# Batch 0 of a linear-attention and MLP kernel: k's first pair loaded ahead of q, w1's first block in row halves, key products by pairs

## The chip, the cores and the metric

The kernel runs on one core of a Trainium2 chip. The metric is device time in microseconds (us) of one execution. Three runs of the kernel before gave 266.63, 266.06 and 266.3 us, median 266.3 us.

Engines are named as in the profile: PE (TensorE, matrix products), PEld (its weight loads), DVE (VectorE), ACT (ScalarE), POOL (GpSimd), SP (SyncE). DMAs are issued from queues of SP, ACT and POOL.

## The reference

```python
q_s = exp(q - max(q, -1)); q_s /= sum(q_s, -1) + 1e-9      # q, k, v: (8, 8, 576, 64), over the head dim
k_s = exp(k - max(k, 2));  k_s /= sum(k_s, 2) + 1e-9       # over the 576 rows
kv  = einsum('bhsd,bhse->bhde', k_s, v)
att = einsum('bhsd,bhde->bhse', q_s, kv)                   # (8, 8, 576, 64)
x   = att.transpose(0, 2, 1, 3).reshape(8, 576, 512)
xn  = (x - mean(x)) / sqrt(var(x) + 1e-6) * g_ln           # over the 512 columns
out = x + relu(xn @ w_ch1) @ w_ch2                         # w_ch1 512 x 2048, w_ch2 2048 x 512
```

Inputs and output are float32.

## The kernel before

The eight batches are worked through in order. Of each, 512 rows make four tiles `t` of 128 rows; the 64 rows that are left of every batch are gathered and make a ninth pass. A pass is an attention part (exponentials on ACT, sums and scalings on DVE, products on PE) and an MLP: `mm1` products with `w1` into `ph`, relu into `hT`, products with `w2` into `pc`, and an output step. While PE works on the MLP of one batch, the attention of the next is laid between its matmuls. The order on every engine is the order in which the code issues instructions: `run(main, side)` walks over the MLP's steps, each with a weight, and issues a side step when the sum of weights has reached the side step's number. From batch 2 on a scheme with seven products in place of eight is used; nothing of it is touched.

Nothing can be laid beside the attention of batch 0, since no MLP is there yet. It is written out by hand in `first_batch` (lines 892 to 993):

- **Loads.** SP issues `load_q0(0)`, which is the half of q for tiles 0 and 1 (L905, 512 KB), then k in four pieces of 288 KB (L916). Piece `j` holds the two heads of pair `j`, with nine rows to a partition. POOL issues v in three pieces (L935: pairs 0 and 1, pair 2, pair 3), the other half of q, then `w1` in two pieces of 256 columns (`w_raw` in the profile, L93) and three of 512, then `w2`, then batch 1.
- **Queries.** `exp_qt(0, t)` on ACT (L198); `norm_q` on DVE (sum L207, reciprocal L250, product L859); `eq_pT` is four transposes on PE into `ptr` (L864) and a copy of `ptr` to `eqT` (L866 on ACT, L868 on DVE).
- **Keys.** `exp_k0(j)` on ACT (L271); `z0_mm(j)`, 18 small matmuls with ones (L279); `recip_z` (L287); `kv0_mm(j)`, 18 small matmuls of the exponentials with v into a PSUM tile `pkv` that two pairs share (L296). Behind the second pair of a tile, two products on DVE write `kv_sb` (L302).
- **Attention out.** `po_half(t, half)` (L402) makes 256 columns of x of tile `t`, from pairs 0 and 1 (`half` 0) or 2 and 3 (`half` 1): two matmuls into `po`, then a copy to `x` on ACT that also sums the row (L407, an ACTIVATE and a read of its accumulator). `sum_halves` adds two such sums on DVE (L414).
- **First x.** `xn_out` on DVE (L380), four transposes (L987), two products with the column `g_col` on DVE into `xnT` (L988). Then comes the first `mm1_part` (L456). `g_columns` (L889, L890) makes `g_col`.
- **warm(n)** issues n matmuls on zeros (L798). Nobody reads what they write.

PSUM has two pools, `att_ps` with two buffers and `mm_ps` with six. A new tile of a pool takes a buffer whose last reader it then waits for. `pkv` and `po_half(t, 0)` are in `att_ps`, `po_half(t, 1)` is in `mm_ps`:

```python
pool, tag = (mm_ps, "m") if half else (att_ps, "a")
po = pool.tile([P, DM], FP32, tag=tag, name="po")
```

The order at the end of the attention part:

```python
recip_z()
for j in range(NP):
    kv0_mm(j)
warm(2)
po_half(0, 0)
warm(3)
po_half(0, 1)
po_half(1, 0)
po_half(1, 1)
sum_halves(0)
```

The MLP of batch 0 begins with matmuls on `w1` columns 0 to 511 and tiles 0 and 1, in `parts` of `mlp_steps`, a tile at a time. Tiles 2 and 3 are made as side steps (`q0_rest`, `x_fast`, `xn_pT`).

Of the kernel before, what the change touches and what calls it, by code (L numbers as in the profile page):

```python
# [12 lines left out]
FP32 = mybir.dt.float32  # L13
# [7 lines left out]
def kernel(  # L21
# [69 lines left out]
    def load_w1(n0, n=512):  # L91
        cols = slice(n0, n0 + n)
        nc.gpsimd.dma_start(w1_sb[:, :, cols], w1_src[:, :, cols])  # L93
# [173 lines left out]
    def exp_k0(j):  # L267

        if j == 0:
            eks[0] = raw.tile([P, NP, T0, D], BF16, tag="kt", name="ek0", bufs=1)  # L270
        nc.scalar.activation(eks[0][:, j], raws[0][0][:, j], AF.Exp)  # L271
# [79 lines left out]
    def po_mm(c, t, i):  # L351


        if i == 0:
            pool, tag = (mm_ps, "m") if c == 0 and t >= 2 else (att_ps, "a")
            pobox["p"] = pobox[c, t] = pool.tile([P, DM], FP32, tag=tag, name="po")
        if c < B:
            nc.tensor.matmul(  # L358
                pobox["p"][:, i * P : i * P + P], eqTs[c][:, t, i, :], kv_sb[:, c, i, :],
                start=True, stop=True,  # L360
            )
        else:
            for half in range(2):
                ps = slice(64 * half, 64 * half + 64)
                nc.tensor.matmul(  # L365
                    pobox["p"][ps, i * P : i * P + P], eqTs[c][:, t, i, ps],
                    kv_sb[:, 2 * t + half, i, :], start=True, stop=True,
                )
# [79 lines left out]
    def mm1_part(c, m, t0, tn, ko):  # L448

        if (m, t0, ko) == (0, 0, 0):  # L450
            new_h()
        half, at = divmod(t0, 2)
        if m % 2 == 0 and at == 0 and ko == 0:
            hbox["ph", m // 2] = mm_ps.tile([P, 2, 2, P], FP32, tag="m", name="ph")
        ph = hbox["ph", m // 2]
        nc.tensor.matmul(  # L456
            ph[:, m % 2, at : at + tn], (w1g if c else w1_sb)[:, ko, m * P : (m + 1) * P],
            xnTs[c][:, t0 : t0 + tn, ko, :],
            start=(ko == 0), stop=(ko == KO1 - 1),
        )  # L460
        if m % 2 == 1 and at + tn == 2 and ko == KO1 - 1:
            dst = hbox["h"][:, m - 1 : m + 1, 2 * half : 2 * half + 2]
            if c == 0 and half and (m // 2) % 2 == 1:
                nc.vector.tensor_scalar_max(dst, in0=ph, scalar1=0.0)
            else:
                nc.scalar.activation(dst, ph, AF.Relu)
# [283 lines left out]
    def mlp_steps(c):  # L750
        if c > FAST:
            return mm1_fast(c) + mm2_fast(c)
        full = range(KO2)
        first, parts = [], ()
        if c == 0:
            full = range(0)
            parts = ((0, 2, 0, 1), (0, 2, 1, 1), (2, 2, 0, 1), (2, 2, 1, 1), (4, 4, 0, 2), (0, 4, 2, 1),
                     (0, 4, 3, 1), (4, 4, 2, 2), (8, 4, 0, 2), (8, 4, 2, 2), (12, 4, 0, 2), (12, 4, 2, 2))
        else:
            full, parts = range(8, KO2), ((0, 8, 0, 2), (0, 8, 2, 2))  # L760
        for m0, mn, t0, tn in parts:
            first += [
                (0.25 * tn, lambda m=m, t0=t0, tn=tn, ko=ko: mm1_part(c, m, t0, tn, ko))
                for m in range(m0, m0 + mn) for ko in range(KO1)
            ]
        first += [(1, lambda m=m, ko=ko: mm1(c, m, ko)) for m in full for ko in range(KO1)]
        if c == 0:
            return first + [
                (1, lambda t=t, ko=ko: mm2_stream(c, t, ko))
                for n in range(4) for t in range(T) for ko in range(4 * n, 4 * n + 4)  # L770
            ]
        if c >= FAST:
            return first + mm2_fast(c)
        return first + [(1, lambda t=t, ko=ko: mm2(c, t, ko)) for t in range(T) for ko in range(KO2)]
# [19 lines left out]
    def warm(n, width=256):  # L794

        w = mm_ps.tile([P, 512], FP32, tag="m", name="warm")
        for _ in range(n):
            nc.tensor.matmul(w[:, 0:width], junk[:, 0:P], junk[:, 0:width], start=True, stop=True)  # L798
# [93 lines left out]
    def first_batch():  # L892

        nc.scalar.preload_act_table_set("natural_log_exp_and_others")
        raws[0] = (
            mlp.tile([P, NP, T0, D], FP32, tag="hT", name="kt0", bufs=1), None,
            raw.tile([P, H, T, D], FP32, tag="qt", name="qt"),
        )
        k0, _, q0 = raws[0]
        v0 = mlp.tile([P, NP, T0, D], BF16, tag="hs", name="v0", bufs=1)  # L900
        raws["v0"] = v0

        def load_q0(half, eng=nc.sync):
            ts = slice(2 * half, 2 * half + 2)
            eng.dma_start(  # L905
                q0[:, :, ts],
                q[0, :, 0:SM, :].rearrange("h (p t) d -> p h t d", t=T)[:, :, ts],
            )

        def src0(x, j, jn):  # L910
            rows = x[0, 2 * j : 2 * j + 2 * jn].rearrange("h (p t) d -> (h p) (t d)", t=T0)
            return rows.rearrange("(j p) n -> p j n", j=jn)

        load_q0(0)
        for j in range(NP):
            nc.sync.dma_start(k0[:, j : j + 1].rearrange("p j t d -> p j (t d)"), src0(k, j, 1))  # L916
        raws["g"] = outp.tile([KO1, P], FP32, tag="ot", name="g_rows")
        nc.scalar.dma_start(
            raws["g"], bass.AP(moe_g_ln.tensor, moe_g_ln.offset, [[P, KO1], [1, P]])
        )  # L920
        nc.vector.memset(junk, 0.0)
        nc.vector.memset(eps_ln, 1e-6)
        nc.vector.memset(ones, 1.0)
        nc.vector.memset(bones, 0.0)
        nc.vector.memset(bones[0:64, 0:1], 1.0)
        nc.vector.memset(bones[64:P, 1:2], 1.0)
        nc.vector.memset(kv_sb, 0.0)
        make_identity(nc, ident)
        nc.gpsimd.tensor_copy(out=ident_f, in_=ident[0:KO1, 0:KO1])
        nc.gpsimd.memset(vr, 0.0)  # L930
        for half in range(2):
            nc.gpsimd.memset(vr[64 * half : 64 * half + 64, :, 4 * half : 4 * half + 4, D:], 1.0)
        nc.gpsimd.memset(vm[:, :, :, :, D:], 1.0)
        for j, jn in ((0, 2), (2, 1), (3, 1)):
            nc.gpsimd.dma_start(  # L935
                v0[:, j : j + jn].rearrange("p j t d -> p j (t d)"), src0(v, j, jn)
            )
        load_q0(1, nc.gpsimd)
        load_w1(0, 256)
        load_w1(256, 256)  # L940
        for nb in range(1, 4):
            load_w1(512 * nb)
        load_w2(0)
        load_w2(1)

        new_eq(0)
        start_x(0)
        warm(31)
        for t in range(2):
            exp_qt(0, t)  # L950
        exp_k0(0)
        exp_k0(1)
        norm_q(0, 0)
        norm_q(0, 1)
        eq_pT(0, 0, nc.scalar)
        g_columns()
        exp_k0(2)
        warm(5)
        z0_mm(0)
        z0_mm(1)  # L960
        exp_k0(3)
        eq_pT(0, 1, nc.vector)
        z0_mm(2)
        warm(3)
        z0_mm(3)
        recip_z()
        for j in range(NP):
            kv0_mm(j)
        warm(2)
        po_half(0, 0)  # L970
        warm(3)
        po_half(0, 1)
        po_half(1, 0)
        po_half(1, 1)
        sum_halves(0)
        exp_qt(0, 2)
        exp_qt(0, 3)
        xn = xs[0][2]
        warm(7)
        for half in range(2):  # L980
            xn_out(0, 0, slice(DH2 * half, DH2 * half + DH2))
        for i in range(2):
            if i:
                warm(2)
            ptr = mm_ps.tile([P, 2, 2 * P], BF16, tag="m", name="ptr")
            for j in range(2):
                nc.tensor.transpose(ptr[:, j, 0:P], xn[:, 0, (2 * i + j) * P : (2 * i + j + 1) * P], ident)  # L987
            nc.vector.tensor_mul(  # L988
                xnTs[0][:, 0, 2 * i : 2 * i + 2], ptr[:, :, 0:P],
                g_col[:, 2 * i : 2 * i + 2].to_broadcast([P, 2, P]),  # L990
            )
        sum_halves(1)
        xn_out(0, 1)
# [36 lines left out]
    with tc.manual_schedule(  # L1030
# [10 lines left out]
        def po_x(c, t):  # L1041
            for i in range(NP):
# [4 lines left out]
            mlp_steps(0),  # L1047
            [
                (2, lambda: (eq_pT(0, 2, nc.scalar), xn_pT(0, 1, nc.vector), eq_pT(0, 3, nc.scalar))),
                (2, lambda: (q0_rest(2), x_fast(0, 2))),  # L1050
                (6, lambda: q0_rest(3)),
                (8, lambda: (xn_pT(0, 2, nc.vector), x_fast(0, 3))),
                (16, lambda: xn_pT(0, 3, nc.vector)),
                (22, lambda: square_sum(0, 0)),
                (26, lambda: square_sum(0, 1)),
# [72 lines left out]
```

## Time and profile before

| | |
|---|---|
| median of three runs | 266.3 us |
| the profiled execution | 266.63 us, of which the span from first to last instruction is 264.8 us and 1.8 us lie around it |
| granted TensorE clock, mean over the span | 0.999 |
| PE busy | 257.6 us, 97% of the span |
| DVE, ACT, POOL busy | 217.0, 175.1, 90.4 us |
| first matmul of the MLP starts | 14.96 us |
| first matmul with w2 starts | 31.53 us |

Times inside the execution are microseconds from the start of the span. In the timeline a row is: start, length, engine, line, operation, what it writes and reads, how many in a row, and in brackets the time that the engine sat idle before it and what ended that. A matmul row's length takes in the drain of its last matmul, so the next row can start before it ends.

### The profile page before, as it was taken

The page shows a single profiled execution, that of the slowest core. Times are in us where ns is not written, and L with a number is a line of the kernel's source. Part 1 is how long each engine was busy: PE and PEld are TensorE (multiplying, and loading weights), DVE is VectorE, ACT ScalarE, POOL GpSimd, SP SyncE. Part 2 cuts the span into 40 slices and gives each one's busy share as a digit, 9 for nine tenths or more (in the row PEclk, how much of TensorE's full clock was granted, in tenths as well). Part 3 has the DMA queues.
Part 4 walks back from the last instruction along what each step waited for, and adds up shares of the span by engine and source line. Part 5 has one row for each costly group of instructions (what it writes and reads, how often), then busy time and mean ns, then how long its engine had stood idle before and what let it go on. Part 6 is the DMA issues. An engine that isn't in the chain of part 4 may idle for free. (4 is left out here: it accounts for less than half of the span.)

```text
span 264.8 us, 6827 instructions
## 1 busy us (share of the span) xinstructions
PE 257.6 (97%) x2708; PEld 217.5 (82%) x2711; DVE 217.0 (82%) x465; ACT 175.1 (66%) x346; POOL 90.4 (34%) x144
## 2 busy tenths in 40 slices
PE   8999999999999999999999999999999999999993
PEld 5778755775988998889888988998899888888882
DVE  4577697968989996999699968996999789877873
ACT  4467851996966886678667866886678378438400
POOL 8742216303059208900880049307300800030000
PEclk9999999999999999999999999999999999999999
DMA  7999999987987995899789997997804530512014
GB/s 226 252 205 207 342 209 329 262 132 255 184 149 221 291 139 101 222 286 143 98 243 268 125 113 235 294 126 155 257 5 84 120 118 5 78 80 81 0 42 119
DMA packets 82328, 45.01 MB, mean 170 GB/s; under 512 B 58036, under 2 KB 78520, under 8 KB 82296
## 3 DMA queue, kind: packets, MB, share of 16 engines
q0 software_dynamic: 32800, 22.29, 45.8%
q1 hardware_dynamic: 48896, 21.76, 40.5%
q10 hardware_dynamic: 600, 0.53, 0.6%
q8 instruction: 21, 0.34, 0.5%
q14 instruction: 11, 0.09, 0.1%
HBM read 36.70 MB, written 9.44 MB: 174 GB/s over the span
## 5 line engine op out<-in xcount | busy, mean ns | idle before, releaser
L548 PEld LDWEIGHTS <-hs 128*128 128x128 bf16 x512 | 49.5, 98 | 5.7
L693 PEld LDWEIGHTS <-w_q 128*128 128x128 bf16 x448 | 43.0, 98 | 6.4 <-issue 1.1
L245 POOL TENSOR_TENSOR tq<-xnT 128x256 bf16<-128x256 bf16 x24 | 15.6, 665 | 76.6 <-DMA xnT<-xn 76.6
L548 PEld LDWEIGHTS <-hT 128*128 128x128 bf16 x384 | 37.2, 98 | 4.4
L693 PEld LDWEIGHTS <-w1g 128*128 128x128 bf16 x336 | 32.2, 98 | 3.9
L548 PE MATMUL ba<-w_q,hs 128*128 128x256 bf16 x256 | 31.7, 273 | 0.0
L693 PE MATMUL bx<-tq,w_q 128*128 128x256 bf16 x224 | 29.4, 272 | 0.2 <-ACT s L721 0.2
L372 ACT ACTIVATE scrap<-x,mv 128x512 bf16<-128x512 bf16 x36 | 25.9, 719 | 1.7 <-DVE x L388 1.3
L717 ACT COPY bc<-bx 128x512 f32<-128x512 f32 x28 | 15.2, 594 | 16.8 <-PE bx L693 16.8
L388 DVE SCALAR_TENSOR_TENSOR x<-po,rq 128x512 bf16<-128x512 f32 x34 | 23.3, 685 | 2.4 <-PE po L358 2.3
L565 POOL DMA_DIRECT2D out_dram<-ot x28 | 15.4, 556 | 24.1 <-DVE ot L559 24.0
L735 ACT ACTIVATE hT<-bc 128x512 bf16<-128x512 f32 x28 | 15.3, 595 | 12.4 <-PE bc L693 12.4
L207 DVE TENSOR_REDUCE zq<-eq 128x16 f32<-128x1024 bf16 (+1 forms) x20 | 20.6, 1049 | 2.0 <-ACT eq L198 2.0
L532 DVE TENSOR_TENSOR hs<-hT 128x1024 bf16<-128x1024 bf16 x32 | 21.3, 674 | 0.9 <-ACT hT L735 0.5
L724 DVE TENSOR_TENSOR bb<-bx,s 128x512 f32<-128x512 f32 x28 | 18.2, 694 | 4.1 <-ACT s L721 4.0
L735 ACT ACTIVATE hT<-bb 128x512 bf16<-128x512 f32 x28 | 15.2, 595 | 9.2 <-PE bb L693 9.2
L358 PE MATMUL po<-kv_sb,eqT 128*128 128x128 bf16 x120 | 20.5, 219 | 0.0
L727 DVE TENSOR_TENSOR hT<-bx,s 128x512 bf16<-128x512 f32 x28 | 18.0, 685 | 2.8 <-PE bx L693 2.8
L573 ACT COPY s<-ba 128x512 f32<-128x512 f32 x15 | 8.7, 579 | 12.5 <-PE ba L548 7.8
L548 PE MATMUL ba<-w_sb,hT 128*128 128x256 bf16 x128 | 16.7, 273 | 0.0
L548 PE MATMUL bb<-w_q,hs 128*128 128x256 bf16 x128 | 16.6, 273 | 0.0
L501 PE MATMUL pc<-w_sb,hT 128*128 128x512 bf16 x61 | 15.8, 379 | 0.2
(135 smaller groups left out, 541.1 us busy)
## 6 DMA issues: line engine op xcount, KB each, us to landing
out_dram<-ot POOLq DMA_DIRECT2D x32, 256.0 KB, 5.6
qt<-in_q_dram SPq DMA_DIRECT2D x5, 1024.0 KB, 6.3
kt<-in_k_dram SPq DMA_DIRECT2D x5, 1024.0 KB, 12.8
w_sb<-in_moe_w_ch_dram POOLq DMA_DIRECT2D x4, 512.0 KB, 16.4
qt<-in_q_dram POOLq DMA_DIRECT2D x2, 1024.0 KB, 14.6
kt<-in_k_dram POOLq DMA_DIRECT2D x2, 1024.0 KB, 14.5
vm<-in_v_dram POOLq DMA_DIRECT2D x16, 128.0 KB, 13.2
w_raw<-in_moe_w_ch_dram POOLq DMA_DIRECT2D x3, 512.0 KB, 12.8
```

The costliest lines, as they stand in the source:

```text
L207: nc.vector.reduce_sum(eqs[c][1][:, ts], eqs[c][0][:, ts], axis=AX.X)
L245: eng.tensor_tensor(out=dst[:, t], in0=x[:, t], in1=y[:, t], op=ALU.subtract)
L358: nc.tensor.matmul(pobox["p"][:, i * P : i * P + P], eqTs[c][:, t, i, :], kv_sb[:, c, i, :], start=True, stop=True,)
L372: nc.scalar.activation(scrap, x[:, t], AF.Square, bias=mv[:, t, 0:1], scale=-float(DM), accum_out=mv[:, t, 1:2],)
L388: nc.vector.scalar_tensor_tensor(x[:, t].rearrange("p (h d) -> p h d", h=H), in0=pobox[c, t].rearrange("p (h d) -> p h d", h=H), scalar=1. ...
L501: nc.tensor.matmul(hbox["pc", t], hbox["h"][:, ko, t, :], w2_sb[:, ko, :], start=(ko == 0), stop=(ko == KO2 - 1),)
L532: nc.vector.tensor_tensor(out=dst, in0=x, in1=y, op=op)
L548: nc.tensor.matmul(hbox[bank][:, t], lhsT, rhs, start=first and (own or t == 0) and k == 0, stop=k == KH - 1, skip_group_check=True)
L693: nc.tensor.matmul(dst[:, q], lhsT, rhs, start=first and q == 0 and ko == 0, stop=ko == 1, skip_group_check=True)
L724: nc.vector.tensor_tensor(out=at[g, "b"], in0=at[g, "x"], in1=at[g, "s"], op=ALU.add)
L727: nc.vector.tensor_tensor(out=h_out(g, 1, 1), in0=at[g, "x"], in1=at[g, "s"], op=ALU.add)
L735: nc.scalar.activation(h_out(g, odd, half), at[g, name], AF.Relu)
```

## The change

- SP issues the first piece of k ahead of q's half. ACT takes the exponential of k's pair 0 first, then q's tiles 0 and 1, then the other three pairs in a row; both copies to `eqT` are on ACT and come behind them.
- The first 512 columns of `w1` come as two halves of the rows (256 rows of 512 columns) where they came as two halves of the columns (512 rows of 256 columns). The first `mm1_part` steps follow: for each tile, the first two row blocks of all four column blocks, then the other two. The `start` flag is changed to go with that.
- On PE: 38 warm matmuls with `g_columns` among them in place of 31; the four `z0_mm` almost in a row; the second `eq_pT` behind them; then the order quoted below.
- In the side steps `q0_rest(2)` and `q0_rest(3)` go from 2 and 6 to 4 and 8. The `po` tiles of tiles 2 and 3 go from `mm_ps` to `att_ps`.

```diff
         if i == 0:
-            pool, tag = (mm_ps, "m") if c == 0 and t >= 2 else (att_ps, "a")
-            pobox["p"] = pobox[c, t] = pool.tile([P, DM], FP32, tag=tag, name="po")
+            pobox["p"] = pobox[c, t] = att_ps.tile([P, DM], FP32, tag="a", name="po")
...
-            start=(ko == 0), stop=(ko == KO1 - 1),
+            start=(ko == 0 and (c > 0 or half > 0 or m >= 4 or at == m % 2 == 0)),
+            stop=(ko == KO1 - 1), skip_group_check=True,
...
-            parts = ((0, 2, 0, 1), (0, 2, 1, 1), (2, 2, 0, 1), (2, 2, 1, 1), (4, 4, 0, 2), (0, 4, 2, 1),
+            parts = ((4, 4, 0, 2), (0, 4, 2, 1),
...
+        if c == 0:
+            first += [
+                (0.25, lambda m=m, t=t, ko=2 * kh + ko: mm1_part(c, m, t, 1, ko))
+                for t in range(2) for kh in range(2) for m in range(4) for ko in range(2)
+            ]
...
-        load_q0(0)
         for j in range(NP):
             nc.sync.dma_start(k0[:, j : j + 1].rearrange("p j t d -> p j (t d)"), src0(k, j, 1))
+            if j == 0:
+                load_q0(0)
...
-        load_w1(0, 256)
-        load_w1(256, 256)
+        for kh in range(2):
+            ks = slice(2 * kh, 2 * kh + 2)
+            nc.gpsimd.dma_start(w1_sb[:, ks, 0:512], w1_src[:, ks, 0:512])
...
-        warm(31)
+        warm(24)
+        g_columns()
+        warm(14)
+        exp_k0(0)
         for t in range(2):
             exp_qt(0, t)
-        exp_k0(0)
-        exp_k0(1)
+        for j in range(1, NP):
+            exp_k0(j)
         norm_q(0, 0)
         norm_q(0, 1)
         eq_pT(0, 0, nc.scalar)
-        g_columns()
-        exp_k0(2)
-        warm(5)
         z0_mm(0)
         z0_mm(1)
-        exp_k0(3)
-        eq_pT(0, 1, nc.vector)
+        warm(3)
         z0_mm(2)
-        warm(3)
         z0_mm(3)
+        eq_pT(0, 1, nc.scalar)
         recip_z()
-        for j in range(NP):
-            kv0_mm(j)
+        kv0_mm(0)
+        kv0_mm(1)
         warm(2)
+        kv0_mm(2)
         po_half(0, 0)
-        warm(3)
+        po_half(1, 0)
+        warm(2)
+        kv0_mm(3)
+        warm(5)
         po_half(0, 1)
-        po_half(1, 0)
         po_half(1, 1)
         sum_halves(0)
...
-                (2, lambda: (q0_rest(2), x_fast(0, 2))),
-                (6, lambda: q0_rest(3)),
-                (8, lambda: (xn_pT(0, 2, nc.vector), x_fast(0, 3))),
+                (4, lambda: (q0_rest(2), x_fast(0, 2))),
+                (8, lambda: (q0_rest(3), xn_pT(0, 2, nc.vector), x_fast(0, 3))),
```

## The prediction

> **What bounds the kernel now.** I read the busy table first, then PE's busy time in the stretches behind the start, then the timelines of the first 16 us engine by engine, and last the landings of the loads.
>
> The busy table, and PE in six stretches from 24 to 244 us (columns: stretch, length and busy time, clock, DMA share, GB/s; the last line is the sum):
>
> ```profile
> PE 257.6 (97%) x2708; PEld 217.5 (82%) x2711; DVE 217.0 (82%) x465; ACT 175.1 (66%) x346; POOL 90.4 (34%) x144
> ...
> 24.00:44.00 20.00, 19.78 (x171) 1.00 1.21 276
> ...
> sum 220.00, PE 219.39; mean PE 36.57
> ```
>
> In these 220 us PE idles 0.61 us. Its order is fixed, so whatever moves the first MLP matmul moves the end, and no more than 0.61 us of a delay can be swallowed there. The change touches only what lies ahead of 21 us, and PE's work behind the first MLP matmul is the same. So the question is when that matmul starts. PE's timeline:
>
> ```profile
> 7.24 0.40 PE L864 MATMUL ptr<-ident,eq 128*128 128x128 bf16 x4 [0.78 <-DVE eq L859]
> ...
> 8.53 0.73 PE L279 MATMUL z<-ones,ek 64*64 64x1 bf16 x36
> ...
> 10.64 1.30 PE L296 MATMUL pkv<-v,ek 64*64 64x64 bf16 x72
> 11.87 0.39 PE L798 MATMUL warm<-junk 128*128 128x256 bf16 x2
> 12.10 0.28 PE L402 MATMUL po<-kv_sb,eqT 128*128 128x128 bf16 x2
> 12.21 0.49 PE L798 MATMUL warm<-junk 128*128 128x256 bf16 x3
> 12.68 0.50 PE L402 MATMUL po<-kv_sb,eqT 128*128 128x128 bf16 x6
> ...
> 14.96 0.70 PE L456 MATMUL ph<-xnT,w_raw 128*128 128x128 bf16 x8 [0.31 <-DMA w_raw<-in_moe_w_ch_dram]
> ```
>
> The same stretch on ACT and on DVE:
>
> ```profile
> 4.87 1.15 ACT L198 ACTIVATE eq<-qt 128x512 bf16<-128x512 f32 x2 [2.85 <-DMA qt<-in_q_dram]
> ...
> 12.41 0.38 ACT L407 ACTIVATE x<-po 128x256 bf16<-128x256 f32 x1 [3.00 <-PE po L402]
> 12.69 0.19 ACT L407 ACTIVATION_READ_ACCUMULATOR x<-po 128x1 f32 x1
> ```
> ```profile
> 11.41 1.21 DVE L302 TENSOR_TENSOR kv_sb<-pkv,rzk 64x128 bf16<-64x128 f32 x4 [0.41 <-PE pkv L296]
> 13.49 0.16 DVE L414 TENSOR_TENSOR mv<-st 128x1 f32<-128x1 f32 x1 [0.87 <-ACT x L407]
> 13.69 0.48 DVE L380 TENSOR_SCALAR xn<-x,mv 128x256 bf16<-128x256 bf16 x2
> 14.35 0.76 DVE L988 TENSOR_TENSOR xnT<-ptr,g_col 128x256 bf16<-128x256 bf16 x2 [0.19 <-PE ptr L987]
> ```
>
> To be seen: one chain from q's landing to the first MLP matmul. q, exponential, norm on DVE, transposes at 7.24, the key products up to 11.87, `kv_sb` from 11.41, `po_half(0, 0)` at 12.10, `po_half(0, 1)` at 12.68 as soon as the fourth `kv_sb` product ends at 12.62, then copy, sum, `xn`, transposes, `xnT`. The first product to `xnT` ends at 14.73; PE waits 0.31 us more, until `w1`'s first piece is there. Loads on SP's queue (columns: KB, us from issue to landing), from the issues ahead of 1.4 us:
>
> ```profile
> qt<-in_q_dram SPq DMA_DIRECT2D x1, 512.0 KB, 4.1
> kt<-in_k_dram SPq DMA_DIRECT2D x1, 288.0 KB, 4.4
> ```
>
> q is issued at 0.74 and lands at 4.84, k's pair 0 is issued at 1.27 and lands at 5.67. Pairs 1 and 3 land at 6.2 and 8.0 by the same view; v at 9.4, 10.2 and 10.9; `w1`'s first pieces at 14.9 and 15.7, its third at 18.3.
>
> **Part 1, k's pair 0 ahead of q.** Five SP issues stay five; q's goes behind one of 0.53 us. When it lands no row shows. It can't beat 1.27 + 4.1 = 5.37, its own time from issue; and at 5.67 q and pair 0 were both down before, so their bytes need no longer than that in the other order. I take the middle, 5.52: 0.68 later than now. [...] Pair 0's exponential (0.67 us) costs nothing: the smaller load is first, so it lands no later than 4.84, and the exponential is over by 5.54.
>
> **Part 2, exponentials without a gap.** q's two end 0.68 later (6.70); pairs 1 to 3 follow, pair 3 from its landing at 8.0 to 8.67. Before, they ended at 9.40. The gain is real but is not what PE waits for: DVE's norm of tile 0 ends at 7.19 + 0.68 = 7.87, so the transposes start at 7.92. The 38 warm matmuls end ahead of that (31 end at 6.47, seven more took 0.93 in the row at 13.01, `g_columns` took 0.3: 7.7), so they cost nothing, with 0.2 us of cover.
>
> From there PE is in a row, each from its own rows: transposes 0.33, two `z0_mm` 0.67, three warms 0.43, two more `z0_mm` 0.38 + 0.31, transposes 0.32 (norm 1 ends at 9.42, ahead of 10.04), so `kv0_mm(0)` starts at 10.36, against 10.64 now. v's first two pairs are there at 9.4. Two `kv0_mm` are half of 72 matmuls that took 1.23: 0.62, to 10.98. DVE starts 0.15 behind (as 11.26 to 11.41), its first two products take 0.59, and `po_half(0, 0)` comes 0.10 behind that: 11.82. So far 0.28 us are gained.
>
> **Part 3, the new order of `kv0_mm` and `po_half`.** This is where it is lost. `po_half(1, 0)` now comes ahead of `kv0_mm(3)`. Both buffers of `att_ps` are then taken: one by `po_half(0, 0)`, the other by the `pkv` of pairs 2 and 3, which is half written. So `po_half(1, 0)` has to wait until ACT has read `po_half(0, 0)`, and behind it in PE's order stand two warms, `kv0_mm(3)`, five warms and `po_half(0, 1)`, and behind that the whole first x. The price: copy starts 0.31 behind `po_half(0, 0)` (12.10 to 12.41) = 12.13; its accumulator read ends 0.47 later = 12.60; 0.06 to PE = 12.66. Then `po_half(1, 0)` 0.11, two warms 0.23, `kv0_mm(3)` 0.31 = 13.31. DVE 0.15 later, two products 0.59, 0.06 to PE: `po_half(0, 1)` at 14.11, against 12.68. The two products of pairs 2 and 3, which now run straight behind the first two, thus start at 13.46 where they started at 12.03. If ACT frees the buffer at the end of the copy and not of the read, it is 0.28 less.
>
> From `po_half(0, 1)` to the end of the first `xnT` product nothing changes: 14.73 − 12.68 = 2.05 us. With 0.05 to PE the first MLP matmul starts at 16.21, which is 1.25 us later than 14.96.
>
> **Part 4, `w1` in row halves.** Two issues for two on POOL, at the same place. The first half lands at 14.9 if it takes as long as the first 256 columns, or 1.3 us behind q's second half (12.58), 13.9, at the rate of the 512 KB blocks that follow 2.5 us apart. Either is ahead of 16.21: cost nothing, cover 1.3 us, and the 0.31 us wait goes, which 14.73 + 0.05 above has no use of. The third piece (18.3 or earlier) is needed 3.8 us behind the first MLP matmul, at 20.0.
>
> **Part 5, the first MLP steps.** Same matmuls. PE's wait of 0.23 us for `eqT` at 16.56 goes, since 8 more matmuls lie ahead; a wait of about 0.11 for `xn` of tile 1 comes (DVE has it 0.86 us behind the first matmul, PE asks at 0.75). Gain 0.12. The moved `po` tiles take `att_ps` buffers that are long free: nothing.
>
> **Sum.** +1.25 − 0.12 = +1.13 us. The profiled execution took 266.63, so it would take 267.76; that one is 0.33 above the median of its three, so for the median I say 266.3 + 1.1 = 267.4. Bounds: q at 5.37 and the earlier release give +0.70, q at 5.67 gives +1.28.
>
> **The rivals.**
> - *The delay is swallowed* (not slower). PE's 0.61 us of idle between 24 and 244 us would all be waits for loads that a later PE no longer meets: +1.13 − 0.61 = +0.52, 266.8, no measurable change. It decides if the start is late by 1.1 us or less. Against it: they are spread over three stretches, and in the waits two of 0.2 us are put to ACT and DVE, which move with PE. 9%.
> - *`po_half(1, 0)` is not held.* If a buffer is free, it follows at once, and `po_half(0, 1)` comes at 11.82 + 0.65 + 0.80 = 13.27: +0.59, less 0.18 for the wait for `w1` that is in 14.96 already, less 0.12: +0.29, 266.6. The code speaks against it: `pkv` is still to be written. 6%.
> - *The start gets faster.* For 0.53 us less, `po_half(0, 1)` would have to come at 12.4 or earlier, 1.7 us ahead of my sum, and no part of the sum is that loose: 4%.
> - *PE slows down in the new gaps.* PE idles 0.7 us ahead of `po_half(1, 0)` and about 0.3 us at four more places. 31 warms at the start took 5.41 us, which at the row of seven in 0.93 would be 4.1; a second such phase costs 1.3 us: 268.7. Against it: 0.78 us of idle ahead of 7.24 slowed nothing down (five warms behind it took 0.72). 5%. [...]
>
> **How the numbers follow.** My case has 76%, and the likeliest time is its own, 267.4. The range takes in its bounds, the second rival at 266.6 and, above, a q load and handoffs slower than any row here by 1 us: 266.6 to 268.4; the last two rivals, 9% in all, lie outside. About 0.2% (0.53 us) is what a measurement can tell from no change. Faster 4%; within it 15% (the first two rivals); slower 81%.
>
> **What would show it.** In the new trace: q's exponential at about 5.5; transposes at 7.9; `po_half(0, 0)` at 11.8; a wait of PE for ACT ahead of `po_half(1, 0)`; the last two `kv_sb` products a separate group at 13.5; first MLP matmul at 16.2 without a wait for `w1`. I am wrong if `po_half(0, 1)` starts ahead of 13, or if the first MLP matmul is late and the end is not.

## The result, and the profile after

| | before | changed |
|---|---|---|
| median of six executions each | 266.23 us (266.06 to 266.63) | 267.82 us (267.11 to 268.85) |
| ratio | | 1.0055, 95% interval 1.0038 to 1.0071 |
| the profiled execution, its span | 266.63, 264.8 us | 267.34, 265.6 us |
| first matmul of the MLP | 14.96 us | 16.80 us |
| first 128x256 block of `mm1` | 18.78 us | 20.39 us |
| first matmul with `w2` | 31.53 us | 33.14 us |

The change makes the kernel slower by 1.59 us in the medians. In the profiled pair a delay of that size is there before 21 us: the block of 128x256 matmuls, from which on PE is nearly gapless, starts 1.61 us later. Some executions of several kernels have a mean granted clock under 0.995 (268.85 is one, at 0.992) and are 0.4 to 3.9 us longer than the median of the others of their kernel, so the median of the others stands beside that of all.

The busy table of the changed kernel, and PE in the stretches from 24 to 244 us (columns of the second: stretch; then busy time of PE, PEld, DVE, ACT, POOL with counts; clock, DMA share, GB/s; the last line sums the six stretches):

```profile
PE 258.7 (97%) x2717; PEld 218.0 (82%) x2717; DVE 216.0 (81%) x464; ACT 175.6 (66%) x347; POOL 90.3 (34%) x144
...
sum 220.00, PE 219.76 PEld 185.94 DVE 189.49 ACT 157.73 POOL 75.59; mean PE 36.63 PEld 30.99 DVE 31.58 ACT 26.29 POOL 12.60
```

PE idles 0.24 us in these 220, against 0.61 before: of the delay 0.37 us is swallowed in this pair of executions. The two executions differ by 0.71 us only. The remaining 0.5 us is not idle time: from the block to its last matmul PE is busy for 241.26 us before and for 240.75 in the changed kernel, and the profiled execution of before is the slowest of its six. The medians differ by 1.59; where PE stands in the executions that were not profiled is not shown.

PE's timeline of the changed kernel:

```profile
7.97 0.40 PE L869 MATMUL ptr<-ident,eq 128*128 128x128 bf16 x4 [0.18 <-DVE eq L864]
...
10.38 0.76 PE L296 MATMUL pkv<-v,ek 64*64 64x64 bf16 x36
...
11.92 0.27 PE L401 MATMUL po<-kv_sb,eqT 128*128 128x128 bf16 x2
12.75 0.27 PE L401 MATMUL po<-kv_sb,eqT 128*128 128x128 bf16 x2 [0.56 <-ACT x L406]
12.86 0.38 PE L803 MATMUL warm<-junk 128*128 128x256 bf16 x2
13.17 0.47 PE L296 MATMUL pkv<-v,ek 64*64 64x64 bf16 x18
...
14.33 0.38 PE L401 MATMUL po<-kv_sb,eqT 128*128 128x128 bf16 x4
...
16.80 0.61 PE L455 MATMUL ph<-xnT,w_raw 128*128 128x128 bf16 x8 [0.26 <-DVE xnT L997]
```

`po_half(0, 0)` is at 11.92, `po_half(1, 0)` waits for ACT until 12.75, and `kv0_mm(3)` and `po_half(0, 1)` come behind it. ACT, DVE and POOL in the same stretch:

```profile
5.54 1.15 ACT L198 ACTIVATE eq<-qt 128x512 bf16<-128x512 f32 x2 [1.03 <-DMA qt<-in_q_dram]
...
12.22 0.38 ACT L406 ACTIVATE x<-po 128x256 bf16<-128x256 f32 x1 [1.15 <-PE po L401]
12.51 0.19 ACT L406 ACTIVATION_READ_ACCUMULATOR x<-po 128x1 f32 x1
```
```profile
11.18 0.59 DVE L302 TENSOR_TENSOR kv_sb<-pkv,rzk 64x128 bf16<-64x128 f32 x2 [0.83 <-PE pkv L296]
13.68 0.59 DVE L302 TENSOR_TENSOR kv_sb<-pkv,rzk 64x128 bf16<-64x128 f32 x2 [1.91 <-PE pkv L296]
15.14 0.16 DVE L413 TENSOR_TENSOR mv<-st 128x1 f32<-128x1 f32 x1 [0.87 <-ACT x L406]
15.34 0.85 DVE L379 TENSOR_SCALAR xn<-x,mv 128x256 bf16<-128x256 bf16 x2
16.22 0.77 DVE L997 TENSOR_TENSOR xnT<-ptr,g_col 128x256 bf16<-128x256 bf16 x2
```
```profile
15.28 0.89 POOL L115 DMA_DIRECT2D kt<-in_k_dram  x1 [1.16 <-ACT x L406]
```

To be seen: the four `kv_sb` products, one group of 1.21 us before, are now two groups with 1.91 us of idle DVE between them. And the two `xn` products took 0.85 us where they took 0.48: the second ran from 15.54 to 16.19, while POOL issued batch 1's k load from 15.28 to 16.17. The loads on SP's queue that are issued ahead of 1.25 us:

```profile
qt<-in_q_dram SPq DMA_DIRECT2D x1, 512.0 KB, 4.3
kt<-in_k_dram SPq DMA_DIRECT2D x1, 288.0 KB, 3.1
```

Pair 0 is issued at 0.74 and lands at 3.8, q at 1.22 and 5.5.

The start by stages (each is the time from one row to the next; the predicted column is from the prediction's own times):

| stage | before | changed | change | predicted change |
|---|---|---|---|---|
| up to the first transposes | 7.24 | 7.97 | +0.73 | +0.68 |
| to `po_half(0, 0)` | 4.86 | 3.95 | −0.91 | −0.96 |
| to `po_half(0, 1)` | 0.58 | 2.41 | +1.83 | +1.71 |
| to the first MLP matmul | 2.28 | 2.47 | +0.19 | −0.18 |
| to the 128x256 block | 3.82 | 3.59 | −0.23 | −0.12 |
| sum | 18.78 | 20.39 | +1.61 | +1.13 |

### The profile page after: what moved, and what is told of

It is laid out like the page before. It is cut to its first block, busy times and chain, and to the rows that moved or that the text cites. A ratio compares the mean times of both kernels' runs of the same rounds, so it can differ in the third digit from the quotient of the medians.

```text
span 265.6 us, 6843 instructions
## 1 busy us (share of the span) xinstructions
PE 258.7 (97%) x2717; PEld 218.0 (82%) x2717; DVE 216.0 (81%) x464; ACT 175.6 (66%) x347; POOL 90.3 (34%) x144
## 5 line engine op out<-in xcount | busy, mean ns | idle before, releaser
L245 POOL TENSOR_TENSOR tq<-xnT 128x256 bf16<-128x256 bf16 x24 | 15.6, 665 | 79.6 <-DMA xnT<-xn 79.6
## 6 DMA issues: line engine op xcount, KB each, us to landing
qt<-in_q_dram POOLq DMA_DIRECT2D x2, 1024.0 KB, 14.7
```

What stands on the lines that cost most here:

```text
L245: eng.tensor_tensor(out=dst[:, t], in0=x[:, t], in1=y[:, t], op=ALU.subtract)
```

## Experiments

All results, in us; "block" is the start of the 128x256 block in the profiled execution, "of the others" is the median of the executions with a granted clock of 0.995 or more, and the last column counts those under it.

| kernel | first MLP matmul | block | median (n) | of the others | ratio to before, 95% | under 0.995 |
|---|---|---|---|---|---|---|
| changed | 16.80 | 20.39 | 267.82 (6) | 267.72 | 1.0038 to 1.0071 | 1 |
| e1_po_behind | (half clock) | | 267.2 (12) | 267.04 | 1.0023 to 1.0075 | 3 |
| e2_own_buffer | 15.71 | 19.66 | 267.59 (10) | 267.46 | 1.0032 to 1.0066 | 3 |
| e3_keys_together | 15.27 | 19.11 | 266.86 (12) | 266.39 | 1.0008 to 1.0029 | 6 |
| e4_k1_held | 16.51 | 20.52 | 267.87 (6) | 267.85 | 1.0040 to 1.0087 | 1 |
| e5_q_first | 16.82 | 20.43 | 267.89 (8) | 267.88 | 1.0033 to 1.0069 | 1 |
| e6_together_q_first | 14.71 | 18.57 | 266.44 (12) | 266.44 | 0.9985 to 1.0008 | 0 |
| e7_w1_alone | 14.94 | 18.52 | 266.17 (12) | 266.17 | 0.9980 to 1.0005 | 0 |
| e8_more_warm | (half clock) | | 267.1 (12) | 266.41 | 1.0005 to 1.0033 | 7 |
| e9_g_late | 16.25 | 19.99 | 267.6 (12) | 267.59 | 1.0033 to 1.0083 | 2 |
| e10_load_alone | 16.14 | 20.38 | 267.64 (6) | 267.64 | 1.0028 to 1.0064 | 0 |
| e11_held_alone | 17.09 | 20.97 | 268.11 (6) | 268.11 | 1.0041 to 1.0085 | 0 |
| e12_together_g_late | 14.70 | 18.48 | 266.49 (12) | 266.16 | 0.9989 to 1.0030 | 3 |

Before, run beside them on the same chips: medians 266.3 (27), 266.42 (31) and 266.43 (23); 2 of these 81 are under 0.995.

### The held product

The theory was that the wait of `po_half(1, 0)` for a buffer costs most of the time. Four kernels test it: the product moved, the wait taken away, the old order put back, and the new order alone in the kernel before. A clean measure is the time from `po_half(0, 0)` to `po_half(0, 1)`: 0.58 us before, 2.41 in the changed kernel.

**e1_po_behind**

```diff
         po_half(0, 0)
-        po_half(1, 0)
         warm(2)
         kv0_mm(3)
         warm(5)
         po_half(0, 1)
+        po_half(1, 0)
         po_half(1, 1)
```

> The changed kernel with one line moved: po_half(1, 0) behind po_half(0, 1), so that kv0_mm(3) no longer stands behind the wait for ACT. Theory A (the held po_half(1, 0) is the main cost): the last two kv_sb products start at about 12.85 in place of 13.68, po_half(0, 1) comes at 13.5 in place of 14.33, the xn products clear the issue of k's load at 15.28, the first MLP matmul starts at 15.6 in place of 16.80, and the time falls by 1.2 us, to about 266.6. Rival B (the late q load behind k's pair 0 is the main cost): the chain ahead of po_half(0, 0) is untouched, so the time falls by less than 0.4 us.

Median 267.2, and 267.04 without the three executions at a lower clock: 0.6 to 0.7 us are won, half of the 1.2 expected. The profiled execution is one of the three, so its places in the timeline can't be compared, and why it isn't more stays open. But it shows something else. PE by microseconds (columns as above):

```profile
11.00:12.00 1.00, 1.00 (x51) 0.88 (x47) 0.18 (x1) 0.30 (x1) 1.00 (x2) 1.00 1.07 315
12.00:13.00 1.00, 1.00 (x29) 0.53 (x24) 0.53 (x2) 0.29 (x1) 0.83 (x2) 0.57 1.14 205
...
15.00:16.00 1.00, 1.00 (x10) 0.79 (x10) 0.58 (x2) 0.00 (x0) 0.47 (x1) 0.72 1.26 207
```

The granted clock falls to a half from 12.14 for 3.41 us. PE had idled 1.33 us ahead of its transposes, which came at 9.19 in this execution, because q landed at 6.8 here and not at 5.5.

**e2_own_buffer**

```diff
-        pool, tag = (mm_ps, "m") if half else (att_ps, "a")
+        pool, tag = (mm_ps, "m") if half or t else (att_ps, "a")
```

> The changed kernel in its own order, but po_half(1, 0) takes a buffer of mm_ps. Theory A (it is the buffer that holds it): po_half(1, 0) follows po_half(0, 0) at about 12.03 without a wait for ACT, po_half(0, 1) comes at 13.6, the first MLP matmul at 15.7, and the time falls by 1.1 us, nearly as in the run with the line moved. Rival C (not the buffer, but something else that stands in PE's way there, eqT of tile 1 or v's last piece): po_half(1, 0) or kv0_mm(3) still starts late and the time falls by less than 0.3 us.

```profile
11.77 0.38 PE L401 MATMUL po<-kv_sb,eqT 128*128 128x128 bf16 x4
...
13.46 0.38 PE L401 MATMUL po<-kv_sb,eqT 128*128 128x128 bf16 x4
...
19.42 0.40 PE L869 MATMUL ptr<-ident,xn 128*128 128x128 bf16 x4 [0.41 <-DVE xn L379]
```

With a buffer of `mm_ps` the wait is gone: `po_half(1, 0)` follows at once (the first row holds both), `po_half(0, 1)` starts at 13.46, 0.87 earlier than in the changed kernel, and the first MLP matmul 1.09 earlier. From `po_half(0, 0)` it is 1.69 us now, so the wait is 0.72 us of the 1.83 that this stage lost; the other 1.11 are the order itself, in which `kv0_mm(3)` and its two `kv_sb` products come behind `po_half(0, 0)`. And of the 1.09 only 0.73 reach the block, and 0.2 to 0.3 the median, which the runs can't tell from zero (the two intervals in the table overlap). In the profiled pair PE idles 0.27 us more behind the block (0.54 against 0.27 up to 244 us); where the rest went is not shown. What the block loses is a new wait of 0.41, for the `xn` product of tile 2, and its reason is the same collision that the changed kernel has at 15.54:

```profile
18.64 0.72 DVE L379 TENSOR_SCALAR xn<-x,mv 128x512 bf16<-128x512 bf16 x1
```
```profile
18.38 0.89 POOL L139 DMA_DIRECT2D vt<-in_v_dram  x1 [1.67 <-DMA w_raw<-in_moe_w_ch_dram]
```

**e3_keys_together** is the changed kernel with the order of before from `kv0_mm` to `po_half`:

```diff
-        kv0_mm(0)
-        kv0_mm(1)
+        for j in range(NP):
+            kv0_mm(j)
         warm(2)
-        kv0_mm(2)
         po_half(0, 0)
-        po_half(1, 0)
-        warm(2)
-        kv0_mm(3)
-        warm(5)
+        warm(3)
         po_half(0, 1)
+        po_half(1, 0)
         po_half(1, 1)
```

> The changed kernel with the whole stretch from kv0_mm(0) to po_half(1, 1) in the order of the kernel before; loads, exponentials and w1 stay changed. Theory A: kv0_mm runs from 10.4 to 11.6, po_half(0, 1) comes at 12.4 (12.68 before), the first MLP matmul at 14.75 to 14.9 (w1's first half lands at 14.7), and the time is 1.9 us under the changed kernel, 0.1 to 0.3 under the kernel before. Rival B (late q is the main cost): it stays above the kernel before by 0.5 us or more.

`po_half(0, 1)` at 12.59, first MLP matmul at 15.27, 1.53 earlier than in the changed kernel. Median 266.86, and 266.39 for the executions at 0.995 or more: 1.0 to 1.3 us of the 1.6 are the order of the key products. From `po_half(0, 0)` to `po_half(0, 1)` it is 0.52 us, as short as before. Both `xn` products ran beside an issue of POOL here (0.72 and 0.58 us in place of 0.28), which held the first MLP matmul by 0.43.

**e11_held_alone** makes the same exchange the other way round, in the kernel before.

> The kernel before with the new order of the key products and x's halves alone: kv0_mm of pairs 0, 1, 2, then po_half(0,0), po_half(1,0), then kv0_mm(3), po_half(0,1), po_half(1,1), with the warm-ups of the change between them. Loads, exponentials, g_columns and w1's pieces as before. Theory (the order costs by itself, since po_half(1,0) finds both buffers of its pool taken and holds pair 3 behind it): pair 3's key products about 1.3 us behind po_half(0,0), po_half(0,1) at 13.8 to 14.2 in place of 12.68, first MLP matmul at 16.1 to 16.5 with the wait for w1 gone, median 267.3 to 267.7. Rival (the order costs only together with the late load order, which leaves VectorE nothing to do in between): po_half(0,1) within 0.3 us of 12.68, median within 0.3 us of the kernel before's.

```profile
12.22 0.29 PE L402 MATMUL po<-kv_sb,eqT 128*128 128x128 bf16 x2
13.07 0.27 PE L402 MATMUL po<-kv_sb,eqT 128*128 128x128 bf16 x2 [0.56 <-ACT x L407]
...
14.64 0.38 PE L402 MATMUL po<-kv_sb,eqT 128*128 128x128 bf16 x4
```

`po_half(0, 1)` is at 14.64, 1.96 later than before, which is beyond the 13.8 to 14.2 expected, and the median 268.11, 1.7 us slower and no better than the whole change. `po_half(0, 1)` comes 2.43 us behind `po_half(0, 0)`, as in the changed kernel: the order costs by itself.

### The loads and the norm

**e5_q_first** gives q its place ahead of k back, and its exponentials too.

```diff
+        load_q0(0)
         for j in range(NP):
             nc.sync.dma_start(k0[:, j : j + 1].rearrange("p j t d -> p j (t d)"), src0(k, j, 1))
-            if j == 0:
-                load_q0(0)
...
-        warm(14)
-        exp_k0(0)
+        warm(9)
         for t in range(2):
             exp_qt(0, t)
-        for j in range(1, NP):
+        for j in range(NP):
             exp_k0(j)
```

> The changed kernel with q's half loaded and its exponentials taken ahead of k's pair 0 again (and 9 warms in place of 14 behind g_columns, since the transposes come earlier); the order of kv0_mm and po_half stays changed. The load order alone: transposes at about 7.25 in place of 7.97, po_half(0, 0) at 11.1 in place of 11.92, first MLP matmul at 15.7 in place of 16.80. Theory A+B (both the load order and the held po_half(1, 0) cost): the time falls by about 1 us against the changed kernel and stays above the kernel before by 0.3 to 0.6. If v's landing or pair 3's exponential takes the place of q: po_half(0, 0) is not ahead of 11.6 and the time falls by less than 0.5.

A miss: 267.89. q's exponential was at 4.91, but the transposes stayed at 8.00. DVE in this kernel:

```profile
6.22 0.16 DVE L895 TENSOR_SCALAR g_col<-gcp 128x4 f32<-128x4 f32 x1 [2.73 <-PE gcp L894]
6.30 0.68 DVE L207 TENSOR_REDUCE zq<-eq 128x8 f32<-128x512 bf16 x1
```

The norm's first sum stands behind `g_col` in DVE's order; `g_col` waits for a matmul that stands behind 24 warms on PE. These are slow: in the changed kernel the 24 take 4.78 us, 0.20 each, where the seven at 14.55 take 0.93, 0.13 each. In the changed kernel this wait was hidden behind q's later landing (its sum starts at 6.27 too).

**e9_g_late** moves it out of the way (the diff is against e5_q_first):

```diff
         warm(24)
-        g_columns()
         warm(9)
...
         eq_pT(0, 0, nc.scalar)
+        g_columns()
         z0_mm(0)
```

> The changed kernel with q's half loaded and exponentiated ahead of k's first pair (as in the kernel before), nine warm-up matmuls in place of fourteen, and g_columns moved back behind the first transposes, as in the kernel before; the held order of the key products stays. It differs from e5_q_first in the place of g_columns alone. Theory (in e5_q_first it was g_columns, which waits for its matmul behind 24 warm-ups and stands ahead of the norm in VectorE's order, that kept the transposes at 8.00 although q's exponentials ended 0.6 us earlier than in the changed kernel): transposes at 7.2 to 7.4, first eq^T x kv at 11.1 to 11.3, first MLP matmul at 15.6 to 15.9, median 266.9 to 267.2, so 0.7 to 1.0 us under e5_q_first. Rival (something else bounds the norm, or k's pair, now second, makes the key products late in place of it): transposes or key products within 0.2 us of e5_q_first's, median 267.7 to 268.0.

The transposes came at 7.30, as expected, so the hold by `g_col` is shown. But `po_half(0, 0)` came at 11.59 and not 11.2: the matmul of `g_columns` now stands between the transposes and `z0_mm`, where PE has no gap, and takes 0.31 there. The first MLP matmul was at 16.25, 0.57 earlier than in e5_q_first. The median moved by 0.3 us only, less than expected, with intervals that overlap.

**e6_together_q_first** is e5_q_first with the key products in the order of before (the edit of e3_keys_together):

> Both undone: q first as in the run above, and kv0_mm and po_half in the order of the kernel before; w1 in halves of the rows and the exponentials of k without a gap stay. po_half(0, 1) at about 12.0 (12.68 before), then the first MLP matmul waits for w1's first half at 14.7: it starts at 14.75 against 14.96 before. Theory A+B: the time is at or up to 0.3 us under the kernel before. If w1 in row halves or the moved side steps cost by themselves: above it by 0.3 or more.

266.44, ratio 0.9985 to 1.0008: no difference to the kernel before. `po_half(0, 1)` is at 11.89, 0.79 earlier than before, but PE idles 0.68 ahead of the first MLP matmul, until `w1` is there at 14.71; so only 0.24 us are left of the 0.79, and the median shows none of it.

**e12_together_g_late** has the late `g_columns` as well:

> All that the runs so far spoke against is taken out of the changed kernel: q's half first, g_columns behind the first transposes, key products and x's halves in the order of before. What is left of the change: exponentials of k without a gap, w1's first block in row halves with the pieces of the MLP reordered, the scores' buffers and the side steps. Theory (w1's first row half, which lands at 14.7, then bounds the start): transposes at 7.2 to 7.4, po_half(0,1) at 11.5 to 12.0, first MLP matmul at 14.7 to 14.9 after a wait for w_raw of 0.5 us or more, the 128x256 block at 18.4 to 18.6, median 266.0 to 266.4, within 0.2 us of the kernel before's. Rival (the earlier attention side pays): first MLP matmul at 14.3 or earlier, median 265.8 or less.

```profile
14.70 0.62 PE L455 MATMUL ph<-xnT,w_raw 128*128 128x128 bf16 x8 [0.38 <-DMA w_raw<-in_moe_w_ch_dram]
```

266.49 (266.16 for the executions at 0.995 or more), again the time of before. What the rest of the change wins ahead of 14.7 ends at the landing of `w1`'s first half. In this execution both `xn` products also ran beside an issue of POOL (0.60 and 0.47 us), so that `w1` held the start by some 0.1 us only; in e6_together_q_first it was 0.4.

**e10_load_alone** is the kernel before with only k's pair 0 ahead of q, the exponentials without a gap and 36 warms for 31:

> The kernel before with the load order and the exponentials of the change alone: k's first pair ahead of q's half on the queue, its exponential first, the others behind q's without a gap, 36 warm-up matmuls in place of 31 ahead of the first transposes; g_columns, the order of the key products and w1's pieces stay as before. Theory (the prediction's: q 0.68 us later moves everything up to the first MLP matmul by that): transposes at 7.9 to 8.0, first eq^T x kv at 12.3 to 12.8, first MLP matmul at 15.3 to 15.6 with its 0.31 us wait for w1 gone, median 266.6 to 266.9. Rival (the exponentials without a gap and the earlier keys give it back): first MLP matmul within 0.2 us of 14.96, median within 0.2 us of the kernel before's. If this load order is what brings executions with a granted clock under 0.995 (23 of 56 in the five kernels with k's first pair first, 1 of 32 in those with q first, 0 of 58 of the kernel before), one or more of its executions shows it; if it takes the earlier exponentials together with g_columns ahead, none does.

267.64, slower than expected by 0.7 us or more. Transposes at 7.89 and `po_half(0, 0)` at 12.75, each 0.65 later than before, as the theory had it. What it hadn't is this row:

```profile
16.02 0.23 PE L988 MATMUL ptr<-ident,xn 128*128 128x128 bf16 x1 [0.77 <-issue]
```

PE stopped for 0.77 us ahead of the last transpose of `xn`, whose data had been there since 14.82, waiting for nothing that the profile shows. No other kernel here has such a row in its trace. A read of 16 KB on the instruction queue ran from 13.51 to 14.45. But the kernel before has such a read from 12.86 to 13.82 and the changed kernel from 12.61 to 13.50, and PE does not stop there, so the read alone is not the cause. In this execution the block comes 1.60 us later than before, of which 0.65 and 0.77 make up the most. The median is 1.2 us up; whether the executions that were not profiled have the stop too is not shown.

### `w1` in row halves

**e7_w1_alone** is the kernel before with the change's `w1` halves, its order of the first MLP steps, its side steps and buffers of `po`.

```diff
-        load_w1(0, 256)
-        load_w1(256, 256)
+        for kh in range(2):
+            ks = slice(2 * kh, 2 * kh + 2)
+            nc.gpsimd.dma_start(w1_sb[:, ks, 0:512], w1_src[:, ks, 0:512])
```

> The kernel before with only the w1 part of the change: row halves, the new first MLP steps, the later side steps, the po tiles in att_ps. Its 0.31 us wait for w1 should shrink by 0.2 us, to the landing of the first half (14.7), and the 0.23 us wait for eqT should go: 0.2 to 0.4 us under the kernel before. If the row halves don't land earlier or xn of tile 1 is late for its new place: within 0.1 us.

```profile
14.94 0.61 PE L455 MATMUL ph<-xnT,w_raw 128*128 128x128 bf16 x8 [0.28 <-DVE xnT L994]
```

266.17, ratio 0.9980 to 1.0005: no difference that can be told from zero, though the block starts 0.26 earlier. This part costs nothing, as predicted. But the wait of 0.31 did not shrink by 0.2, as expected: with `w1`'s half there, the first MLP matmul starts 0.02 us earlier, and PE now idles 0.28 for `xnT`. The wait that the profile put down to `w1` before was hardly `w1`'s.

### The product on DVE beside POOL's DMA issue

**e4_k1_held** holds batch 1's k load by a small copy on POOL until the first `xnT` is there:

```diff
-        load_behind(1, (2, 0))
+        load_behind(1, (2,))
+        alloc(1, (0,))
+        nc.gpsimd.tensor_copy(out=raws[1][0][0:1, 0, 0, 0:4], in_=xnTs[0][0:1, 0, KO1 - 1, 0:4])
+        load_behind(1, (0,))
```

> The changed kernel with one small POOL copy ahead of the load of batch 1's k: the copy waits for the first xnT, so POOL's issue of that load moves from 15.28 to about 16.7, away from the second xn product on DVE. That product took 0.65 us in the changed kernel, from 15.54 to 16.19, while POOL issued from 15.28 to 16.17; its like took 0.3 in the kernel before. Theory D (POOL's issue slows the DVE product beside it): it takes 0.3 us, the first MLP matmul starts at about 16.4 in place of 16.80, and the time falls by 0.3 to 0.4 us. Rival (the length has another cause, the exponentials on ACT beside it or where the product stands): it keeps its 0.65 us and the time stays within 0.15 us.

Both `xn` products took 0.48 together, and the first MLP matmul came 0.29 earlier (0.07 of it because `po_half(0, 1)` was earlier in this execution). But the next issue of POOL moved too, and hit the product of tile 2:

```profile
19.45 0.78 DVE L379 TENSOR_SCALAR xn<-x,mv 128x512 bf16<-128x512 bf16 x1
```
```profile
19.25 0.89 POOL L139 DMA_DIRECT2D vt<-in_v_dram  x1 [0.23 <-DMA w_raw<-in_moe_w_ch_dram]
```

PE waits 0.47 there, the block starts at 20.52, and the median is 267.87: the 0.3 to 0.4 us expected are not won. The collision is shown; as a remedy the copy fails. Over the first 25 us of all traces of this study, a product that started 0.20 us or more into such an issue didn't end before the issue did: 0.46 to 0.72 us for 256 columns (0.28 alone), 0.61 to 0.78 for 512 (0.35 alone), in all 12 cases where it would have ended earlier. One that started up to 0.17 us into it wasn't touched (nine cases). The products into `xnT`, which read PSUM, kept their time (0.77 for two beside an issue, 0.76 alone). What ties the two engines together there is not shown.

### More warm-up matmuls

**e8_more_warm** is e3_keys_together with four more warms ahead of tile 0's `xn` transposes and three behind them:

> The run e3_keys_together with seven more warm matmuls where its trace shows PE idle ahead of the first MLP matmul (11 in place of 7 ahead of the first transposes of xn, 3 ahead of the first MLP matmul). In 6 of 12 runs of e3 the mean granted clock was 0.990 or 0.991, and these took 0.6 us more than the other six. Theory E (PE's idle stretches at the start let the clock drop for a few us in some runs): fewer runs at a clock under 0.995, and a median 0.3 us under that of e3. Rival (the drop hangs on when the execution starts, or lies elsewhere in the run): the same share of slow-clock runs and the same median.

267.1, with seven of twelve executions under 0.995 (six in e3_keys_together): the warms in these places do not help. In the profiled execution the granted clock is a half from 11.65 us for 6.83 us, so the new warms, from 16.78 on, come when the drop has begun. PE had idled 0.69 and 1.12 us ahead of it, because the third and the last piece of k landed at 9.4 and 10.96 us, in place of 7.6 and 8.4 in the changed kernel.

## Why the prediction was right

The sign, the main cause and the range were right; the likeliest time, 267.4, was 0.4 us short of 267.82. The start was put at 1.13 us later and came 1.61 later, so 0.48 are missing in the sum. One row of the kernel before, which the account needs, is the first of the two products to `xnT` by itself:

```profile
14.35 0.42 DVE L988 TENSOR_TENSOR xnT<-ptr,g_col 128x256 bf16<-128x256 bf16 x1 [0.19 <-PE ptr L987]
```

- **q's landing.** Said 5.52, with 5.37 and 5.67 as ends; q landed at 5.51 and its exponential started at 5.54. The middle was a choice between two ends, so that it hit is in part luck: of the seven traces with k's pair 0 first, six have q at 5.43 to 5.55 and one (e1_po_behind) at 6.79. Pair 0, issued 0.48 us ahead of q, landed 1.7 us ahead of it; the upper end, 5.67, was 0.16 late.
- **Transposes to `po_half(0, 0)`.** Said 7.92, 10.36, 11.82; measured 7.97, 10.38, 11.92. The warms had 0.18 us of cover where 0.2 was said. That `g_columns` costs nothing held for this kernel alone: e5_q_first showed that DVE would have waited for it until 6.2 whatever q did. So the prediction's step "q 0.68 later moves the transposes by 0.68" was right in size, but q was not the only thing in that place.
- **The held product.** Said 0.84 behind `po_half(0, 0)`; measured 0.83. The lower bound, a release at the end of ACT's copy, does not fit: the copy ended at 12.60, the read of the accumulator at 12.70, and the product started at 12.75. From there to `po_half(0, 1)` the sum was 0.13 too short: two warms took 0.31 and not 0.23, and the 18 matmuls of `kv0_mm(3)` 0.40 and not 0.31. Of the 1.83 us of this stage, the wait is 0.72 and the later `kv0_mm(3)` 1.11 (e2_own_buffer); by the prediction's own sums with and without the wait it would have been 0.84 and 0.87. So the price was right, but the wait, on which Part 3 puts the loss, is the smaller part of it.
- **"Nothing changes from `po_half(0, 1)` to the first `xnT`."** This is the step that failed, by 0.37 of the 0.48 us. It was put at 2.10 us up to the first MLP matmul, and took 2.47. Of the difference 0.15 was wrong for the kernel before too. As the row above shows, the first product to `xnT` ended at 14.78 and not at 14.73 (the 0.76 us of the merged row are two products that overlap), and the first MLP matmul starts 0.15 us behind that end and not 0.05: the whole way takes 2.25 us in each of the four traces where neither a load nor a product slowed by an issue stands in it (e2, e4, e7, e9). So the 0.31 us that PE idled before, put down to `w1`, were worth only 0.03. The other 0.22 is new: the second `xn` product took 0.65 us beside POOL's issue and not 0.28, and the first product to `xnT`, whose transposes were done at 15.97, had to wait behind it on DVE until 16.22. The prediction looked at what waits for what, and no wait links the product and the issue; before, no `xn` product was slowed by an issue (0.36 us at most for 512 columns in the whole trace), so no row of that trace showed the price.
- **`w1` and the first MLP steps.** The halves landed at 14.7 and 15.6, ahead of need, and cost nothing (e7_w1_alone). The gain was 0.23, not 0.12: the wait for `eqT` went, and the wait for `xn` of tile 1 that was to take its place did not come. This miss made up for a part of the others.
- **The rivals.** *Swallowed*: 0.37 us in the profiled pair; the medians differ by 1.59, about the whole delay of the block. *Not held*: e2_own_buffer made it true; the price of 266.6 given for it was too low by 0.9 (267.46 to 267.59). Its block comes 0.59 later than by that sum: 0.41 is the wait for `xn` of tile 2 that is shown there, 0.24 the later `kv0_mm(3)` (1.11 and not 0.87) and 0.15 the end of the way, told above, less 0.2 of small gains. *Slower PE*: not in the profiled execution, whose clock is 1.00 from 5.17 to 264 us, but such a phase is real: e1_po_behind shows one of 3.41 us at half the clock, where PE's longest idle time ahead of it was 1.33 us, and one of the six executions of the changed kernel has a clock of 0.992.

What stays open: why executions with a lower clock come so often in the changed kernel and its variants (27 of 102) and not in the kernel before (2 of 81) or with one part of the change in it (0 of 24: e7, e10, e11). In both profiled executions with a half clock (e1, e8) a load of SP's queue had landed more than 1 us late, and PE idled 1.33 and 1.12 us for it; but in e11_held_alone PE idled 1.20 us ahead of 7.40 and the clock stayed at 1.00, so the length of the idle time does not settle it. Nor is it the load order alone: 5 of the 24 executions of e9_g_late and e12_together_g_late, which load q first, have it, and the 6 of e10_load_alone, which has none, are too few to tell. Open too is the stop of 0.77 us in e10_load_alone, and so what the load order alone would cost without it. The parts do not add up: alone, the loads cost 1.2 us and the held order 1.7, together with the rest 1.6. That the change also shortens the way from the transposes to `po_half(0, 0)` by 0.91 would account for it, but no run has that part by itself.

## What to carry to other kernels

Before an engine that takes its instructions in the order of issue, as PE does in these traces, is given one that waits for a buffer, count the buffers of its pool that are free at that moment; here the independent `kv0_mm(3)`, queued behind, paid for the wait (0.72 us, for a product that nobody needed yet). Count also what is put behind it by the new order itself (here 1.11 us more). An order that follows the landing of data wins only up to the next landing: ahead of 14.7 us, 0.8 us of earlier attention (e6_together_q_first) moved the first MLP matmul by 0.24 us and the median by nothing, because `w1` was not there. A wait's length in the profile is not what its cause costs: before, 0.31 us stood beside `w1`, and 0.03 of it were `w1`'s. When a stretch is shifted in time, look also at what will now run beside it on engines that it doesn't wait for.

## What was not expected of the hardware

- A bf16 product on VectorE from SBUF to SBUF that started 0.20 us or more into a DMA issue on GpSimd, and would have ended within it, lasted until that issue ended, in all 12 cases in the first 25 us of these traces: 0.65 in place of 0.28 us in the changed kernel, 0.78 in place of 0.35 at most.
- The granted clock fell to a half for 3.41 us after PE idled 1.33 us at most at a stretch (e1_po_behind).
- PE stopped for 0.77 us with no wait that the profile shows (e10_load_alone).
